# Retention attention with two MoE layers: two plain steps in layer 0, single-bank PSUM tiles, set differences in wide pieces, copies ahead of halves, later spills

## The chip, the core and the metric

The kernel runs on one core of one Trainium2 chip. The metric is the device time of one execution in microseconds (us); the median of three runs of the kernel before is 580.47 us (580.2 to 581.05).

## The reference, cut to what matters

```python
for t in range(S):                       # attention: B 2, H 8, S 768, D 64
    state = gamma * state + einsum('bhd,bhe->bhde', k[:, :, t], v[:, :, t])
    y[:, :, t] = scale * einsum('bhd,bhde->bhe', q[:, :, t], state)
x = y.transpose(0, 2, 1, 3).reshape(1536, 512)
h = x @ moe_w_in                          # 512 x 2048
x = (h * (1 / (1 + exp(-h)))) @ moe_w_out # layer 0, 2048 x 512
h = x @ moe2_w_in
out = maximum(0.01 * h, h) @ moe2_w_out   # layer 1
```

## The kernel before

Line numbers are those of the kernel before, whose code stands at the end of this section.

**Order.** The whole program is written by hand for one core (`manual_schedule`): each engine, and SyncE's DMA queue, takes its instructions in the order in which the code issues them. So an instruction that waits holds back everything behind it on its engine.

**Precision.** Each fp32 number is carried as two parts. `halves` (L177) makes them: ScalarE writes the high part h as a rounded copy (L178), then VectorE writes the low part l = s - h (L179). Each product takes three matmuls (`TERMS`: hh, hl, lh).

**Attention** (to about 58 us). Twelve chunks j of 128 positions. One turn of the loop (L537) gives TensorE `scores(j+1)` (L244), which needs queries that GpSimd has scaled (L222, for j of 5 and above), and `values(j)` (L264, L273, and L281 for the running state), which needs the scores that VectorE has masked (`masked`, L251). `store_x(j)` then splits the result y into halves for the up stage. Chunks 3 to 5 and 9 to 11 belong to the second half of a token group: `put_second` splits them in two pieces and forms on VectorE, chunk by chunk, the differences that Strassen's form needs (L318, L319, into `big`). `rest_t` (L324, L325) forms the other two on GpSimd. The table `behind` puts the preparation of the first weight blocks into the loop: `words` (ScalarE L131, L133), `clamp` (VectorE L137, L141), `sign` (L148), `low` (L155), then `split_a`.

**Layer, up stage.** Eight steps, one for each weight block. A step makes four output blocks g of two lanes (p0 and p1, 384 columns each). Step 0 is computed plainly by `begin` (96 matmuls, L648). Steps 1 to 7 take the Strassen-Winograd form (`rest`): 7 products of 12 matmuls (84, L376). They need sums of weight blocks (`sums`, GpSimd L175, then `split_s`) and of tokens (`split_t`, tiles tt0 and tt1). In a step several products accumulate into the same PSUM tile X, which ScalarE copies between them (`copy`, L405: tiles c0 to c2), and VectorE adds the copies to other tiles (`add`, L409). ScalarE applies the activation (`act`, L418 and L420). `keep` (L425) spills a step's g to DRAM.

**Layer, down stage.** Three sets of 512 tokens, each 8 times 24 matmuls of 512 columns (L453). A step's g is fetched back (`fetch_g`, L441) and split (`split_g`). Layer 0's result goes through `finish_x` (`put_first`, `put_second`) into the tiles that layer 1 reads.

**PSUM** is four pairs, p0 to p3, of two banks each. A pair is one tile: whoever waits for it waits for both banks.

## Time and profile before

| | |
|---|---|
| median of three runs | 580.47 us |
| the profiled execution | 580.35 us |
| its span | 578.6 us |
| TensorE (PE) busy | 555.2 us, 96% |
| VectorE (DVE) busy | 342.6 us, 59% |
| ScalarE (ACT) busy | 282.7 us, 49% |
| GpSimd (POOL) busy | 104.4 us, 18% |
| mean granted TensorE clock | 0.987 of full speed |

The profile lists the instructions of each engine with start and duration. The text in brackets at the end of a row says how long the engine had been idle before and who released it. PEclk is the granted clock of TensorE as a share of 2.4 GHz; 0.50 is 1.2 GHz.

### The profile page before, as it was taken

To read this page: it belongs to the slowest core of one execution; us is meant where nothing else is said; L and a number is where in the kernel's file an instruction comes from. 1 tells how busy PE (TensorE), PEld (TensorE's weight loads), DVE (VectorE), ACT (ScalarE), POOL (GpSimd) and SP (SyncE) were. 2 spreads that over 40 slices of the span, in tenths; PEclk is the share of its full clock that TensorE was granted. 3 is DMA by queue.
4 is the path that set the end of the run, shared out by engine and by line. 5 is a ranking of instruction groups with operands and counts; after the bars stand their busy time and mean duration, and the time that the engine had idled before them with its cause. 6 is when DMAs were issued, how large, how long until landed. Compare 5 with 4: busy or idle time off the path is not lost.

```text
span 578.6 us, 7971 instructions
## 1 busy us (share of the span) xinstructions
PE 555.2 (96%) x3246; PEld 498.1 (86%) x3246; DVE 342.6 (59%) x354; ACT 282.7 (49%) x330; POOL 104.4 (18%) x94
## 2 busy tenths in 40 slices
PE   8887979999998999999999899999999999999997
PEld 6776979999997888888888799999998888888885
DVE  4888866888865486676673756666655562212300
ACT  2223566777766565634622565566665453213201
POOL 2675433333300000000200532222200000000000
PEclk9988979999999999999999999999999999999999
DMA  8973216687876957878582075777627782532401
GB/s 323 392 269 116 73 36 219 228 290 283 289 257 237 374 188 215 292 228 311 189 260 105 0 261 175 249 258 252 223 110 290 283 293 94 167 109 84 137 0 73
DMA packets 35129, 119.09 MB, mean 206 GB/s; under 512 B 3218, under 2 KB 3346, under 8 KB 33044
## 3 DMA queue, kind: packets, MB, share of 16 engines
q1 hardware_dynamic: 34800, 118.24, 58.8%
q8 instruction: 25, 0.41, 0.3%
q10 hardware_dynamic: 292, 0.34, 0.2%
q14 instruction: 12, 0.10, 0.1%
HBM read 80.82 MB, written 37.75 MB: 205 GB/s over the span
## 4 chain that ended last, share of the span: by engine, by line
PE 83%; DVE 6%; DMA 5%; ACT 3%; POOL 1%; issue 1%; SPq 0%; DVEq 0%; ACTq 0%
PE p L453 44%; PE p L376 33%; DMA sf<-g 3%; DMA att_a<-att_dram 3%; PE p L648 2%; DVE w L179 2%; POOL sf L175 1%; PE p L273 1%; PE p L264 1%; ACT w L178 1%; PE p L244 1%; DVE c L251 1%; DVE r L155 1%; DVE big L318 1%; DVE big L319 1%
## 5 line engine op out<-in xcount | busy, mean ns | idle before, releaser
L376 PE MATMUL p<-tt,w 128*128 128x384 f32 x672 | 126.3, 340 | 3.7 <-ACT c L405 3.7
L376 PEld LDWEIGHTS p<-tt,w 128*128 128x128 f32 x672 | 119.4, 190 | 5.3 <-ACT c L405 5.2
L179 DVE TENSOR_TENSOR w<-c,w 128x1024 fp32r<-128x1024 f32 x46 | 56.2, 1224 | 90.2 <-ACT w L178 90.1
L453 PE MATMUL p<-w,wt 128*128 128x512 f32 x432 | 98.4, 389 | 0.0
L453 PE MATMUL p<-wt,w 128*128 128x512 f32 x432 | 98.4, 389 | 0.0
L453 PEld LDWEIGHTS p<-wt,w 128*128 128x128 f32 x432 | 81.1, 188 | 16.8
L453 PEld LDWEIGHTS p<-w,wt 128*128 128x128 f32 x432 | 81.1, 188 | 16.8
L178 ACT ACTIVATE w<-c 128x1024 fp32r<-128x1024 f32 x46 | 48.4, 1061 | 60.0 <-DMA c<-g 34.4
L453 PE MATMUL p<-w,w 128*128 128x512 f32 x288 | 67.3, 391 | 1.8 <-DVE w L179 1.0
L376 PE MATMUL p<-xa,w 128*128 128x384 f32 x336 | 64.3, 341 | 2.1 <-ACT big L418 2.1
L453 PEld LDWEIGHTS p<-w,w 128*128 128x128 f32 x288 | 53.8, 188 | 14.3 <-DVE w L179 2.2
L376 PEld LDWEIGHTS p<-xa,w 128*128 128x128 f32 x336 | 59.8, 190 | 2.5 <-ACT big L418 2.5
L409 DVE TENSOR_TENSOR big<-p,c 128x768 f32<-128x768 f32 x42 | 40.1, 954 | 32.3 <-PE p L376 19.8
L405 ACT ACTIVATE c<-p 128x768 f32<-128x768 f32 x42 | 34.1, 812 | 48.7 <-PE p L376 48.6
L175 POOL TENSOR_TENSOR sf<-r 128x256 f32<-128x256 f32 x28 | 33.9, 1232 | 115.6 <-DVE r L155 61.1
L133 ACT ACTIVATE u<-ws 128x1024 int32<-128x1024 uint32 x32 | 36.4, 1137 | 22.5 <-DVE r L155 22.5
L155 DVE CUSTOM_DVE_ANT_0 r<-r,u 128x2048 uint16<-128x2048 uint16 x32 | 41.2, 1289 | 0.9 <-ACT u L133 0.5
L131 ACT ACTIVATE r<-ws 128x1024 f32<-128x1024 f32 x32 | 36.6, 1143 | 9.7 <-DMA scr<-r 5.5
L179 DVE TENSOR_TENSOR w<-sf,w 128x1024 fp32r<-128x1024 f32 (+1 forms) x18 | 21.7, 1205 | 32.8 <-ACT w L178 32.8
L148 DVE SCALAR_TENSOR_TENSOR r<-ws,r 128x1024 int32<-128x1024 int32 x32 | 39.6, 1236 | 0.7
L324 POOL TENSOR_TENSOR big<-big 128x768 f32<-128x768 f32 x4 | 7.3, 1832 | 169.1 <-DVE big L319 169.1
L179 DVE TENSOR_TENSOR w<-r,w 128x768 fp32r<-128x768 f32 (+1 forms) x20 | 23.5, 1175 | 14.5 <-ACT w L178 14.5
(86 smaller groups left out, 566.0 us busy)
## 6 DMA issues: line engine op xcount, KB each, us to landing
ws<-w_dram SPq DMA_DIRECT2D x64, 512.0 KB, 5.7
g<-big SPq DMA_DIRECT2D x16, 1536.0 KB, 5.8
c<-g SPq DMA_DIRECT2D x46, 512.0 KB, 6.8
att_a<-att_dram SPq DMA_DIRECT2D x18, 512.0 KB, 6.4
scr<-r SPq DMA_DIRECT2D x18, 512.0 KB, 6.4
r<-scr SPq DMA_DIRECT2D x18, 512.0 KB, 7.4
att_b<-att_dram SPq DMA_DIRECT2D x6, 512.0 KB, 8.3
out_dram<-big SPq DMA_DIRECT2D x11, 256.0 KB, 2.1
```

Source lines behind the costliest of these rows:

```text
L131: nc.scalar.activation(out=r.bitcast(F32), in_=t[:, :, :, 1].bitcast(F32), func=AF.Abs)
L133: nc.scalar.activation(out=u, in_=t[:, :, :, 0].bitcast(U32), func=AF.Copy, scale=2.0 ** -29)
L148: nc.vector.scalar_tensor_tensor(out=r, in0=t[:, :, :, 1], scalar=-0x40000000, in1=r, op0=ALU.bitwise_and, op1=ALU.bitwise_or)
L155: nc.vector.tensor_tensor(out=r, in0=r, in1=u, op=ALU.add)
L175: nc.gpsimd.tensor_tensor(out=o, in0=a, in1=b, op=op)
L178: nc.scalar.activation(out=h, in_=s, func=AF.Copy)
L179: nc.vector.tensor_tensor(out=l, in0=s, in1=h.bitcast(F32), op=ALU.subtract)
L376: nc.tensor.matmul(out=o, lhsT=a[:, ta, k * 128:k * 128 + 128], rhs=rhs(p, tb, k), start=(begin and m == 0), stop=(end and m == 5), skip_g ...
L405: nc.scalar.activation(out=ct[n][:, c, 0:N], in_=self.X[:, c, 0:N], func=AF.Copy)
L409: nc.vector.tensor_tensor(out=self.block(f, half, lanes), in0=t[:, c, 0:N], in1=ct[n][:, c, 0:N], op=ALU.add)
L453: nc.tensor.matmul(out=y, lhsT=l, rhs=r, start=(i == 0 and f == 0 and n == 0), stop=(i == Q - 1 and f == 1 and n == 2),)
L648: nc.tensor.matmul(out=places[m][:, p, 0:N], lhsT=a[:, ta, r, k * 128:k * 128 + 128], rhs=x, start=(n_ == 0), stop=(n_ == 11), skip_group_ ...
```

## The change

**1. A second plain step.** Step 1 of layer 0 is plain as well (96 matmuls in place of 84). `plain` takes the place of `begin`. Its g goes into `big`, and step 0's g into the three c tiles, which the new `keep` spills in step 1. Product 1 of the next step and the copy of it come ahead of the last plain block.

**2. PSUM.** Pairs 2 and 3 become four single banks b0 to b3 (`bank`, `lanes_of`). In the attention y and the state's u lie in separate banks, and `state(j)` is issued between the halves. An `add` into the single banks is made of two instructions of 384 columns in place of one of 768, so each Strassen-Winograd step has six of them for three.

**3. Set differences.** The subtractions L318 and L319 go from `put_second`. `first_t` and `rest_t` make them for all three chunks at once (128x768). In layer 0 lane 0's four are on GpSimd, right behind the attention's last `queries`, and lane 1's on VectorE in steps 0 and 1. In layer 1 lane 0's are on GpSimd in the down stage before, and lane 1's in step 0, two on VectorE and two on GpSimd.

**4. Copies first.** `finish_x` has ScalarE copy the results out of PSUM whole, and the halves are made later from the copies in SBUF. In the attention ScalarE copies chunks 5 and above to `big` behind their halves (in the kernel before only those of the first half, L350).

**5. Last step of a layer.** Its products run in the order 6, 2, 7, 5, 4, 3 (before: 6, 2, 5, 7, 4, 3). The first g is fetched in step 6 and the second in the last step, step 6's spill comes behind the last step, and the first g is split early in the last step. One weight block's preparation goes from layer 1's step 0 to layer 0's down stage.

```diff
+    call = sb.tile([128, 3, 2, 512], F32, name="c")
+    ct = [call[:, i] for i in range(3)]
...
+    def bank(i):
+        return ps.tile([128, 512], F32, tag=f"b{i}", name=f"b{i}")
+
+
+    def lanes_of(i):
+        if i < 2:
+            t = pair(i)
+            return [t[:, 0], t[:, 1]], [(slice(0, 2), t)]
+        t = [bank(2 * i - 4), bank(2 * i - 3)]
+        return t, [(slice(n, n + 1), t[n].unsqueeze(1)) for n in range(2)]
...
+    PLAIN = ((0, 0, 0), (0, 0, 1), (1, 0, 0))
...
-        t = pair(2 + j % 2)
-        yu[j] = y, uu = t[:, 0], t[:, 1]
+        yu[j] = y, uu = bank(2 * (j % 2)), bank(2 * (j % 2) + 1)
...
-    def put_first(s, a, b, ys):
...
-        f, t = xf[p][:, :, :, a:b], tm[p][:, :, :, a:b]
-        h, l = (xb[p][:, n, :, a:b] for n in range(2))
-        halves(*(t[:, :, a:b] for t in b12[p]), ys[0])
...
-        nc.vector.tensor_tensor(out=t[:, 0], in0=ys[0], in1=f[:, 0], op=ALU.subtract)
-        nc.vector.tensor_tensor(out=t[:, 1], in0=ys[1], in1=t[:, 0], op=ALU.subtract)
-        halves(h, l, ys[1])
-
...
+
+
+    def first_t(p, e):
         f, t = xf[p], tm[p]
-        nc.gpsimd.tensor_tensor(out=f[:, 0], in0=t[:, 1], in1=f[:, 0], op=ALU.subtract)
-        nc.gpsimd.tensor_tensor(out=f[:, 1], in0=f[:, 1], in1=t[:, 1], op=ALU.subtract)
+        e.tensor_tensor(out=t[:, 0], in0=t[:, 0], in1=f[:, 0], op=ALU.subtract)
+        e.tensor_tensor(out=t[:, 1], in0=t[:, 1], in1=t[:, 0], op=ALU.subtract)
+
+    def rest_t(p, e):
+        f, t = xf[p], tm[p]
+        e.tensor_tensor(out=f[:, 0], in0=t[:, 1], in1=f[:, 0], op=ALU.subtract)
+        e.tensor_tensor(out=f[:, 1], in0=f[:, 1], in1=t[:, 1], op=ALU.subtract)
...
-        kept = False
+        y = g4(y)
+        f = (tm if s % 2 else xf)[s // 2][:, :, :, a:b]
...
+        if s % 2 == 0:
+            halves(*(xa[s // 2][:, n].rearrange("p (a k) n -> p a k n", a=2)[:, :, :, a:b] for n in range(2)), y)
+            state(j)
...
-            put_second(s, a, b, [y[:, 0], y[:, 1]])
+            halves(*put(s, a, b, 0)[0:2], y[:, 0])
+            state(j)
+            halves(*put(s, a, b, 1)[0:2], y[:, 1])
+        if j >= LATE:
+            nc.scalar.activation(out=f, in_=y, func=AF.Copy)
...
+        def go(self, n):
+            if n == 1:
+                self.X = lanes_of((self.i + self.layer) % 2)
+            if n == 2:
+                self.Z = lanes_of(2)
+            if n == 5:
+                self.V = lanes_of(3)
+            t = {2: "Z", 5: "V", 3: "V"}.get(n, "X")
+            for p, o in enumerate(getattr(self, t)[0]):
+                product(n, self.w, p, o[:, 0:N], n in (1, 2, 5), n in (2, 3, 4))
...
+        def add(self, f, half, n, t):
+            for c, t in t[1]:
+                nc.vector.tensor_tensor(
+                    out=self.block(f, half, c), in0=t[:, :, 0:N], in1=ct[n][:, c, 0:N], op=ALU.add
+                )
...
+            nc.sync.dma_start(out=t.rearrange("p f (s n) -> p f s n", s=4), in_=self.g)
...
+        for k, y in ((1, yb), (0, ya)):
+            for lo, hi, n, a in segments:
+                h, l, f = put(n, a, a + hi - lo, k)
+                for c, t in y[1]:
+                    nc.scalar.activation(out=f[:, c], in_=t[:, :, lo:hi], func=AF.Copy)
+                later.append((n, lambda h=h, l=l, f=f: halves(h, l, f)))
+        return [f for _, f in sorted(later, key=lambda t: t[0])]
...
         behind = {
-            2: lambda: load_next(), 5: lambda: load_next(),
+            2: load_next, 5: load_next,
             4: lambda: words(wa), 6: lambda: clamp(wa), 7: lambda: signed(wa),
-            8: lambda: low(wa), 9: lambda: split_a(wa),
-            10: lambda: (rest_t(0), words(wb)), 11: lambda: (rest_t(1), clamp(wb), signed(wb)),
+            8: lambda: low(wa), 9: lambda: split_a(wa), 10: lambda: words(wb), 11: lambda: clamp(wb),
...
             store_x(j)
-            state(j)
...
                 if k == 0:
-                    at(0, lambda: split_t(0, 0), lambda: low(wb))
-                    at(1, lambda: sums(wb), lambda: split_t(1, 0))
-                    at(2, lambda: split_a(wb))
-                    at(3, lambda: split_t(0, 1), lambda: words(wc))
-                    at(4, lambda: split_s(wb))
-                    at(5, lambda: split_t(1, 1))
+                    at(0, lambda: signed(wb), lambda: first_t(0, nc.gpsimd), lambda: rest_t(0, nc.gpsimd))
+                    at(1, lambda: low(wb))
+                    at(2, lambda: split_a(wb), lambda: words(wc))
+                    at(3, lambda: first_t(1, nc.vector))
+                    at(4, lambda: split_t(0, 0))
+                    at(5, lambda: split_t(1, 0))
                     at(6, lambda: clamp(wc), lambda: signed(wc))
                     at(7, lambda: low(wc), lambda: sums(wc))
                 else:
-                    at(0, lambda: split_a(wc))
-                    at(1, lambda: split_s(wc), lambda: words(wd))
-                    at(2, lambda: clamp(wd))
-                    at(3, lambda: signed(wd))
-                    at(4, lambda: low(wd), lambda: sums(wd))
+                    at(0, lambda: split_t(0, 1), lambda: rest_t(1, nc.vector))
+                    at(2, lambda: split_a(wc), lambda: words(wd))
+                    at(3, lambda: split_s(wc))
+                    at(4, lambda: split_t(1, 1), lambda: clamp(wd))
+                    at(5, lambda: signed(wd))
+                    at(6, lambda: low(wd), lambda: sums(wd))
...
             if k == 0:
-                at(0, lambda: split_t(1, 0), lambda: fetch_w(n))
-                at(2, lambda: split_a(n), lambda: words(w))
-                at(4, lambda: sums(n), lambda: clamp(w))
-                at(5, lambda: signed(w), lambda: fetch_w(m))
-                at(6, lambda: split_s(n), lambda: split_t(1, 1))
-                at(7, lambda: sums(m), lambda: (low(w), keep_w(w)))
+                at(0, lambda: fetch_w(n), lambda: first_t(1, nc.vector), lambda: rest_t(1, nc.gpsimd))
+                at(1, lambda: split_a(n))
+                at(2, lambda: split_t(1, 0))
+                at(4, lambda: sums(n), lambda: fetch_w(m))
+                at(6, lambda: split_s(n))
+                at(7, lambda: split_t(1, 1), lambda: sums(m))
...
-        def begin(s, n, tasks, tags, second_half, put_back):
+        def plain(s, n, before, tasks, tags, order, put_back):
...
+                    if before and p == 0 and at == 1:
+                        before.keep()
+                    f, half = ((0, 0), (1, 0), (0, 1), (1, 1))[m]
...
+                    for c, t in y[m][1]:
+                        if c.stop == p + 1:
+                            s.act(f, half, [(c, t)])
+                    if n and p == 1 and at == 2:
+                        n.go(1)
+                        n.copy(0)
                 put_back[p]()
-            n.go(1)
-            n.copy(0)
...
         def rest(s, n, before, tasks):
-            seq = (6, 2, 5, 7, 1, 4, 3) if n else (6, 2, 5, 7, 0, 4, 3)
+            seq = (6, 2, 5, 7, 1, 4, 3) if n else (6, 2, 7, 5, 4, 3)
             for m, p in enumerate(seq):
                 if m == 2:
-                    if before.i:
+                    if before.w not in PLAIN:
                         before.act(0, 1)
-                    before.keep()
-                if p == 7:
+                    if n:
+                        before.keep()
+                    else:
+                        fetch_g(s.layer, 0, 1)
+                if m == 3:
...
+                if m == 3:
                     s.add(1, 1, 2, s.V)
...
             for k in range(Q):
                 tasks = up_tasks(layer, k)
                 s, n = steps[k], steps[k + 1]
-                if k == 0:
-                    begin(s, n, tasks, ((0, 1, 2, 3), (1, 3, 0, 2))[layer],
-                          ((1, 0, 2, 3), (2, 0, 1, 3))[layer], put_back)
+                if s.w in PLAIN:
+                    more = n.w in PLAIN
+                    plain(s, None if more else n, steps[k - 1] if k else None, tasks,
+                          ((0, 1, 2, 3), (1, 3, 0, 2))[layer], ((0, 1, 2, 3), (0, 2, 1, 3))[layer],
+                          [lambda: None] * 2 if more else put_back)
                     s.done()
                     continue
                 if n is None:
                     ahead = second_w[layer][:2]
-                    tasks[2] += [lambda: fetch_g(layer, 0, 0), lambda: fetch_g(layer, 0, 1)]
-                    tasks[3] += [lambda: fetch_w(ahead[0])]
-                    tasks[4] += [lambda: split_g(layer, 0, 0), lambda: fetch_g(layer, 0, 2)]
-                    tasks[5] += [lambda: fetch_w(ahead[1])]
-                    tasks[6] += [lambda: split_g(layer, 0, 1)]
+                    tasks[1] += [lambda: split_g(layer, 0, 0)]
+                    tasks[2] += [lambda: fetch_w(ahead[0])]
+                    tasks[4] += [lambda: fetch_g(layer, 0, 2), lambda: fetch_w(ahead[1]), lambda: split_g(layer, 0, 1)]
+                elif k == Q - 2:
+                    tasks[4] += [lambda: fetch_g(layer, 0, 0)]
                 rest(s, n, steps[k - 1], tasks)
+            steps[Q - 2].keep()
             steps[Q - 1].act(0, 1)
             fetch_g(layer, 0, 3)
             steps[Q - 1].keep()
...
-                    finish_x(s, ya, yb)
-                    if s:
-                        rest_t(s - 1)
+                    later = finish_x(s, ya, yb)
+                    if s < 2:
+                        for m, f in enumerate(later):
+                            todo[n + 1 + m // 2].append(f)
+                    else:
+                        for f in later:
+                            f()
+                    if s == 1:
+                        todo[n + 3] += [lambda: first_t(0, nc.gpsimd), lambda: rest_t(0, nc.gpsimd)]
...
```

VectorE, attention, from the low words of the first weight block (L155 before, L167 now) to the masked scores of chunk 11 (the second L251 or L265); w1 and xb1 take chunk 9's halves, w2 the weight's. Before:

```order
L155 ISA r0_74<-r0_74,u_77 128x2048
L251 TENSOR_TENSOR c1_70<-p0_544,c0_69 128x1024
L179 TENSOR_TENSOR w1_87<-p3_555,w1_87 128x2x128
L318 TENSOR_TENSOR big_68<-p3_555,big_68 128x2x128
L319 TENSOR_TENSOR big_68<-p3_555,big_68 128x2x128
L179 TENSOR_TENSOR xb1_67<-p3_555,xb1_67 128x2x128
L294 TENSOR_TENSOR gst_84<-gst_84,p3_555 128x256
L179 TENSOR_TENSOR w2_88<-r0_74,w2_88 128x1024
L251 TENSOR_TENSOR c2_71<-p1_591,c0_69 128x1024
```

Now:

```order
L167 ISA r0_72<-r0_72,u_75 128x2048
L265 TENSOR_TENSOR c_69<-p0_546,c_69 128x1024
L191 TENSOR_TENSOR w1_85<-b2_557,w1_85 128x2x128
L307 TENSOR_TENSOR gst_82<-gst_82,b3_558 128x256
L191 TENSOR_TENSOR xb1_67<-b2_557,xb1_67 128x2x128
L191 TENSOR_TENSOR w2_86<-r0_72,w2_86 128x1024
L265 TENSOR_TENSOR c_69<-p1_593,c_69 128x1024
```

The two subtractions are gone and the state update (L294, now L307) stands ahead of the second half; the weight's low part still stands ahead of the masked scores.

TensorE at the change from plain blocks to the first Strassen-Winograd step of layer 0; its first product is p1_794 before and p0_911 now. Before:

```order
L648 MATMUL p3_664<-w1_87,w2_88 128x384 x6
L648 MATMUL p3_664<-xb1_67,w2_88 128x384 x6
L376 MATMUL p1_794<-xa0_64,w3_89 128x384 x6
L376 MATMUL p1_794<-xa1_65,w3_89 128x384 x6
L376 MATMUL p1_794<-tt0_85,w4_659 128x384 x6
L376 MATMUL p1_794<-tt1_658,w4_659 128x384 x6
```

Now:

```order
L654 MATMUL b1_795<-w1_85,w3_87 128x384 x6
L654 MATMUL b1_795<-xb1_67,w3_87 128x384 x6
L381 MATMUL p0_911<-xa0_64,w4_654 128x384 x6
L381 MATMUL p0_911<-xa1_65,w4_654 128x384 x6
L654 MATMUL b3_797<-w1_85,w3_87 128x384 x6
L654 MATMUL b3_797<-xb1_67,w3_87 128x384 x6
L381 MATMUL p0_911<-tt0_83,w5_655 128x384 x6
L381 MATMUL p0_911<-tt1_653,w5_655 128x384 x6
```

The first product's 12 matmuls moved ahead of the last plain block, which lies between them and the product with tt0.

ScalarE in the last up step of layer 0; sf holds the first g that is fetched back, r2 a weight block of the down stage. Before:

```order
L405 ACTIVATE c2_71<-p1_1492 128x2x384
L178 ACTIVATE w0_86<-r2_76 128x1024
L178 ACTIVATE w1_87<-sf_78 128x1024
L418 ACTIVATE big_68<-big_68 128x2x384
L418 ACTIVATE big_68<-p1_1492 128x2x384
L178 ACTIVATE w2_88<-c0_69 128x1024
```

Now:

```order
L413 ACTIVATE c_69<-p1_1532 128x2x384
L143 ACTIVATE r2_74<-ws1_71 128x1024
L145 ACTIVATE u_75<-ws1_71 128x1024
L190 ACTIVATE w5_655<-sf_76 128x1024
L426 ACTIVATE big_68<-big_68 128x2x384
L413 ACTIVATE c_69<-p1_1532 128x2x384
L426 ACTIVATE big_68<-big_68 128x2x384
L190 ACTIVATE w2_86<-r2_74 128x1024
L190 ACTIVATE w0_84<-c_69 128x1024
```

The split of the first g moved ahead of two activations, of the last copy and of the weight's split.

## Rows read from the trace of the kernel before

**Rows 1.** Waits of TensorE: who waited for whom, us, times, longest.

```profile
PE p L264 <- DVE c L251: 7.0, 4, 2.8
```

**Rows 2.** TensorE in time order, attention: start, us, line, tiles, [idle <-releaser].

```profile
26.97 1.09 PE L264 MATMUL p<-c,att_a 128*64 128x128 f32 x16 [1.33 <-DVE c L251]
...
33.02 1.09 PE L264 MATMUL p<-c,att_a 128*64 128x128 f32 x16 [2.24 <-DVE c L251]
...
46.84 1.09 PE L273 MATMUL p<-att_a,gst 64*64 64x128 f32 x16
...
55.16 1.98 PE L264 MATMUL p<-c,att_b 128*64 128x128 f32 x16 [2.76 <-DVE c L251]
57.06 1.68 PE L273 MATMUL p<-att_b,gst 64*64 64x128 f32 x16
```

**Rows 3.** TensorE in order of time, around the first Strassen-Winograd products of layer 0.

```profile
77.83 3.44 PE L376 MATMUL p<-xa,w 128*128 128x384 f32 x12 [2.14 <-ACT big L418]
82.18 3.91 PE L376 MATMUL p<-tt,w 128*128 128x384 f32 x12 [0.90 <-ACT c L405]
```

**Rows 4.** TensorE in order of time, ends of both up stages, layer 1.

```profile
181.44 2.35 PE L376 MATMUL p<-tt,w 128*128 128x384 f32 x12 [0.96 <-ACT c L405]
...
186.59 0.49 PE L453 MATMUL p<-w,w 128*128 128x512 f32 x1 [0.70 <-ACT w L178]
187.85 10.99 PE L453 MATMUL p<-w,w 128*128 128x512 f32 x47 [0.76 <-DVE w L179]
...
325.35 1.29 PE L648 MATMUL p<-b,w 128*128 128x384 f32 x6 [2.67 <-DVE xb L179]
...
338.01 2.25 PE L376 MATMUL p<-xa,w 128*128 128x384 f32 x12
341.15 2.38 PE L376 MATMUL p<-tt,w 128*128 128x384 f32 x12 [0.90 <-ACT c L405]
...
438.86 2.35 PE L376 MATMUL p<-tt,w 128*128 128x384 f32 x12 [0.96 <-ACT c L405]
```

**Rows 5.** Stretches: us; PE, PEld, DVE, ACT, POOL busy; PEclk; DMA share; GB/s.

```profile
34.40:37.80 3.40, 3.40 (x40) 2.95 (x38) 1.89 (x3) 1.10 (x3) 2.79 (x4) 0.50 0.89 334
54.90:58.30 3.40, 3.15 (x28) 2.81 (x30) 1.71 (x5) 2.04 (x3) 0.00 (x0) 0.50 0.02 5
78.70:85.60 6.90, 6.00 (x20) 5.49 (x19) 5.51 (x5) 4.14 (x6) 0.65 (x1) 0.51 0.12 36
90.00:170.00 80.00, 80.00 (x459) 79.90 (x458) 65.84 (x69) 60.34 (x70) 24.16 (x20) 1.00 0.74 260
```

**Rows 6.** VectorE in order of time, attention and layer 0's first step.

```profile
46.89 2.20 DVE L155 CUSTOM_DVE_ANT_0 r<-r,u 128x2048 uint16<-128x2048 uint16 x1
49.01 1.21 DVE L251 TENSOR_TENSOR c<-p,c 128x1024 f32<-128x1024 f32 x1
...
51.80 0.43 DVE L179 TENSOR_TENSOR xb<-p,xb 128x256 fp32r<-128x256 f32 x1 [0.45 <-ACT xb L178]
...
52.74 1.23 DVE L179 TENSOR_TENSOR w<-r,w 128x1024 fp32r<-128x1024 f32 x1 [0.20 <-ACT w L178]
...
68.07 1.22 DVE L155 CUSTOM_DVE_ANT_0 r<-r,u 128x2048 uint16<-128x2048 uint16 x1
```

**Rows 7.** GpSimd in order of time, attention.

```profile
27.96 1.28 POOL L222 TENSOR_TENSOR att_b<-att_b,gst 128x512 f32<-128x512 f32 x1 [1.49 <-DMA att_b<-att_dram]
...
46.20 1.81 POOL L324 TENSOR_TENSOR big<-big 128x768 f32<-128x768 f32 x1
47.97 2.80 POOL L325 TENSOR_TENSOR big<-big 128x768 f32<-128x768 f32 x1
```

**Rows 8.** ScalarE in order of time, attention.

```profile
51.38 0.38 ACT L178 ACTIVATE xb<-p 128x256 fp32r<-128x256 f32 x1 [2.41 <-DVE big L319]
51.66 1.05 ACT L178 ACTIVATE w<-r 128x1024 fp32r<-128x1024 f32 x1
```

**Rows 9.** Costliest groups: line, shapes, count, busy us, mean ns, idle before.

```profile
L409 DVE TENSOR_TENSOR big<-p,c 128x768 f32<-128x768 f32 x42 | 40.1, 954 | 32.3 <-PE p L376 19.8
```

More of the change, by code (lines that the diff above doesn't have):

```diff
@@ new lines, in copy, with act @@
+        def copy(self, n):
+            for c, t in self.X[1]:
+                nc.scalar.activation(out=ct[n][:, c, 0:N], in_=t[:, :, 0:N], func=AF.Copy)
+        def add(self, f, half, n, t):
[3 more added lines that the diff above has]
+                )
+        def act(self, f, half, t=None):
+            for c, i in [(slice(0, 2), None)] if t is None else t:
+                o = self.block(f, half, c)
+                i = o if i is None else i[:, :, 0:N]
+                if self.layer == 0:
+                    nc.scalar.activation(out=o, in_=i, func=AF.Silu)
+                else:
+                    nc.scalar.activation(out=o, in_=i, func=AF.Prelu, alpha=0.01)
@@ L541, in retention_moe_kernel @@
             if j == 0:
-                gb = pair(3)[:, 0]
+                gb = bank(2)
                 for r in range(2):
@@ L653, in begin @@
-                    if p == 1:
-                        s.act(f, half, places[m])
+                    todo = [(kk, ta, tb) for kk in range(4) for ta, tb in TERMS]
+                    for i, (kk, ta, tb) in enumerate(todo):
+                        x = xa[p][:, tb, kk] if half == 0 else b12[p][tb][:, kk] if kk < 2 else xb[p][:, tb, kk - 2]
+                        k = kk % 2
+                        nc.tensor.matmul(
+                            out=y[m][0][p][:, 0:N], lhsT=a[:, ta, (A11, A21)[f] + kk // 2, k * 128:k * 128 + 128],
+                            rhs=x, start=(i == 0), stop=(i == len(todo) - 1), skip_group_check=True,
+                        )
@@ L672, in rest @@
                     n.copy(0)
-                elif p:
+                else:
                     s.go(p)
```

128 lines of the change are left out of this document (34 added, 94 removed).

## The prediction

> **What bounds the kernel now.** Read the shares of the engines first: TensorE is busy for 96% of the 578.6 us span, so the end is set by how long TensorE works and by the few places where it waits. The waits of TensorE come next. The largest is the 7.0 us that the attention's value products wait for VectorE's masking, in four pieces [rows 1]. Then TensorE in order of time gives the place of each wait: 1.33, 2.24 and 2.76 us in the attention [rows 2], 2.14 and 0.90 at the first Strassen-Winograd step of layer 0 [rows 3], and in [rows 4] 0.96, 0.70 and 0.76 at the end of layer 0's up stage, 2.67 in layer 1's plain step, 0.90 behind it and 0.96 at the end of layer 1's up stage. Last, the stretches: from 90 to 170 us TensorE is busy for all 80.00 us, 459 matmuls of 0.174 each, with VectorE at 65.84, while in three short stretches the granted clock is at the lower level, 1.2 GHz [rows 5]. The first two of these come just after the waits that end at 33.02 and 55.16, the third during the two waits of [rows 3]. Twelve matmuls of a product take 2.25 us at full clock [rows 4] (at 338.01) and 3.44 and 3.91 in that third stretch [rows 3].
>
> The sum is made against the profiled execution, 580.35 us (span 578.6 and 1.75 around it), 0.12 below the median of the runs.
>
> **Attention.** Without the two subtractions, masked scores 5 and 6 leave VectorE earlier, and y's bank no longer waits for the state's matmuls. The waits of 1.33 and 2.24 go. In place of the second, GpSimd is late: its query product for chunk 7 waits for a transfer until 27.96 and takes 1.28 [rows 7], and TensorE, which would ask at about 28.3 (value products 5, now at 25.6, with the state's products behind them), waits some 0.97. So the chunks behind it come 1.33 + 2.24 - 0.97 = 2.6 us earlier. The lower clock from 34.40 to 37.80 cost half of 3.40 us [rows 5]; since a wait of 0.97 stays, I count half of that back, 0.85. Chunk 9's y, which ended at 46.84 + 1.09 = 47.93 [rows 2], then ends at 44.5.
>
> What is late next is chunk 11. Its masked scores still stand behind the split of the first weight block. From 44.5 the queue runs: ScalarE 0.38, VectorE 0.43, ScalarE 0.38, VectorE 0.43, ScalarE's whole copy (128x512: between 0.38 for 256 columns and 1.05 for 1024, I take 0.6), ScalarE's high part of the weight 1.05, VectorE's low part 1.23, masking 1.21 [rows 6, 8]. That is 5.7, and about 0.5 for hand-overs between the engines: 50.7. New beside it are GpSimd's four wide set differences, 1.81 each by [rows 7], right behind its last query product, so from about 43.5 to 51. Two VectorE operations of this queue read SBUF only: the low words and the weight's low part. Rows show what such a meeting does: the low words at 46.89 beside GpSimd's operation of 46.20 took 2.20, and 1.22 without one at 68.07; the masking at 49.01, whose input is in PSUM, took 1.21 although GpSimd's next operation ran [rows 6, 7]. So a meeting costs 0.98; at worst a whole GpSimd operation, 1.81, at best nothing. Two at 0.98 give 52.7 (bounds 50.7 and 54.3). Value products 11 start at 52.7 instead of 55.16: gain 2.46 (0.86 to 4.46). TensorE is idle longer ahead of them than before, so I leave the lower clock at the end of the attention as it was: 1.98 + 1.68 there [rows 2].
>
> The Trainium skill (SBUF — State Buffer, section "Who interferes with whom") speaks against this step: a VectorE instruction with two SBUF inputs and a GpSimd instruction that reads SBUF share a port pair that one holds for its whole instruction, and the later one is blocked fully. The trace agrees: 46.20 + 1.81 + 1.22 is 49.2, and the low words ended at 49.09; GpSimd's next operation took 2.80, having queued behind them. By this rule each meeting costs between 0 and 1.81, so the attention's gain would lie between the same bounds; without it, it would be 4.46.
>
> **Layer 0, up stage.** Twelve matmuls more: 84 become 96, 12 times 0.174 = +2.1 (2.25 with the fill, [rows 4]). The second plain step needs no sums of its weight block and no split tokens, so 16.7 us more of TensorE (96 times 0.174) go by before the first Strassen-Winograd step asks for any. Its first product waited 2.14 for the activation that frees its PSUM pair, queued on ScalarE behind a split that waited for GpSimd's sums. Now the sums are made well ahead. The pair's last block ends two blocks, 24 matmuls or 4.2 us, before product 1 asks; ScalarE has one activation to fit in, 0.8, at worst behind one token split of 1536 columns (about 1.5 on the line through 0.38 and 1.05 of [rows 8]) and one more activation. So the pair is free 1 to 3 us before TensorE asks. The 0.90 for the copy goes too: a plain block of 12 matmuls (2.1) now lies between product 1 and the next use of X, against a copy of 0.8 (768 columns on the same line). With both waits gone nothing precedes the third stretch of lower clock, so its 3.44 - 2.25 + 3.91 - 2.25 = 2.85 goes. Together 2.1 - 2.14 - 0.90 - 2.85 = -3.79. The bound on the bad side is that the pair comes late; that is a rival below.
>
> **The steady steps.** Six adds of 384 columns stand for three of 768, which took 0.954 each [rows 9]. No row shows 384 columns. Half of 0.954 and all of it are the ends, 0 to +2.9 a step on VectorE. Between 0.43 for 256 and 0.954 for 768 columns a line gives 0.55, which I take: +0.45 a step. A step is 84 times 0.174 = 14.6 us, and VectorE is busy for 65.84 of 80, so 12.0 of it [rows 5]: 2.6 of cover. Cost nothing.
>
> **Last step of layer 0.** With product 5 between 7 and 4 the copy after 7 has 2.1 us of cover: -0.96. The first g is fetched during step 6, so its split no longer waits for the transfer, and the down stage's first operand is ready: -0.70 - 0.76. SyncE's queue takes the first fetch ahead of the spill of step 6; behind it stand two weight fetches and the second fetch, which by the order are used two products or more later. Together -2.42 (bounds 0 and -2.42).
>
> **Layer 1.** Its third plain block waited 2.67 for PSUM that the subtractions and a split held. Six copies on ScalarE, 0.4 to 0.8 each by [rows 8], now free it within about 3.5 us, under two blocks of 4.2: -2.67. What they push back, the halves of the last set, is asked for by lane 1, four blocks or 8.4 us after the start. The 0.90 at 341.15 I leave: the copy now has a block's cover, but stands behind a weight split that waits for GpSimd's two differences and sums (bounds: it goes, -0.90, or grows by a GpSimd operation, +1.8). Its last step gains 0.96 as layer 0's does; I count the start of its down stage as unchanged. Moving the weight words to the down stage costs nothing, ScalarE being idle there.
>
> **Sum.** -2.46 - 3.79 - 2.42 - 2.67 - 0.96 = -12.3. 580.35 - 12.3 = 568.05, and 0.12 for the median: 568.2 us. Its own range is 565.5 to 571.
>
> **Rivals.**
> *Better attention.* No meeting and full clock: 2.0 less by the bound above, and 1.98 + 1.68 - 2 x 1.09 = 1.5 less [rows 2]: 564.7. For it: GpSimd may begin its differences late enough to miss the weight's low part. Against: the idle ahead of value products 11 grows.
> *The pair still late at step 2.* If ScalarE's activation of the second plain step waits for the token split, which itself waits for VectorE's differences beside GpSimd's sums, the wait returns at its old size with its lower clock: 2.14 + 2.85 = 5.0 more, 573.2. For it: that split stands directly ahead of the activation on ScalarE. Against: 1 to 3 us of slack.
> *Slower.* The single-bank adds cost what an operation costs that meets GpSimd, and VectorE sets the pace in layer 0's six Strassen-Winograd steps. At x us an add VectorE's work in a step is 12.0 - 2.86 + 6x; it exceeds 14.6 from x = 0.91, and the result is slower than before from 6 (9.14 + 6x - 14.6) = 12.3, so x = 1.25. At 0.55 + 0.98 = 1.53 it adds 22.3: 590.5. Against: their first input is in PSUM, as that of the masking which no meeting slowed.
> *The change does nothing.* The attention's transfers and the ports take back what the waits gave, and new waits stand at the layer ends: 580. The steps hold separately, so this needs all to fail.
>
> **Chances.** Forecast 0.58, better attention 0.17, pair late 0.17, slower 0.05, nothing 0.03. About 0.2% is what a measurement of this kernel tells from no change. So faster 0.92, same 0.03, slower 0.05. The range that holds the time 8 times in 10 reaches from the better attention to just above the late pair: 563.5 to 574.5.
>
> **What would show it.** Right: value products 11 start near 52.7; no idle before value products 5, 6 and 10, and about 1 us before score products 7; no wait and full clock at the first Strassen-Winograd step; no idle at the start of layer 0's down stage; layer 1's third plain block starts behind the second. Wrong: an idle of TensorE of more than 1 us anywhere between step 2 and the end of layer 0's up stage, adds above 0.9 us, or a stretch of lower clock in the two plain steps.

## The result and the profile after

The changed kernel takes 566.79 us (median of four runs, 566.38 to 569.15) against 580.41 for the kernel before: ratio 0.9772, 95% interval 0.9744 to 0.980. The forecast was 568.2 us, within 563.5 to 574.5. The profiled execution took 566.38, 13.97 less than that of before; the spans differ by 14.0 (578.6 and 564.6).

TensorE's share and instructions, from the page of the changed kernel:

```profile
PE 552.4 (98%) x3258; PEld 496.9 (88%) x3258; DVE 340.2 (60%) x377; ACT 285.9 (51%) x348; POOL 104.2 (18%) x92
```

TensorE in order of time, changed kernel. L258 is the attention's score products, L277 and L286 its value products, L654 the plain steps, L381 the Strassen-Winograd products, L458 the down stage:

```profile
29.08 1.16 PE L258 MATMUL p<-att_b 64*128 64x128 f32 x16 [0.79 <-POOL att_b L236]
...
41.82 1.16 PE L258 MATMUL p<-att_a 64*128 64x128 f32 x16 [0.96 <-POOL att_a L236]
...
51.53 1.09 PE L277 MATMUL b<-c,att_b 128*64 128x128 f32 x16 [2.72 <-issue]
...
54.19 5.42 PE L654 MATMUL p<-xa,w 128*128 128x384 f32 x24
59.45 1.23 PE L654 MATMUL b<-w,w 128*128 128x384 f32 x6
...
86.68 2.25 PE L381 MATMUL p<-xa,w 128*128 128x384 f32 x12
...
90.88 2.24 PE L381 MATMUL p<-tt,w 128*128 128x384 f32 x12
...
131.26 2.35 PE L381 MATMUL p<-tt,w 128*128 128x384 f32 x12 [0.40 <-ACT c L413]
...
176.35 2.35 PE L381 MATMUL b<-xb,w 128*128 128x384 f32 x12 [0.82 <-DVE big L417]
178.54 1.52 PE L458 MATMUL b<-w,w 128*128 128x512 f32 x6
...
195.67 1.20 PE L458 MATMUL b<-w,wt 128*128 128x512 f32 x4 [0.20 <-DVE wt L191]
...
207.70 1.20 PE L458 MATMUL b<-w,wt 128*128 128x512 f32 x4 [0.64 <-DVE wt L191]
...
310.74 2.25 PE L654 MATMUL p<-xa,w 128*128 128x384 f32 x12
...
314.90 1.20 PE L654 MATMUL p<-b,w 128*128 128x384 f32 x6
...
329.54 2.25 PE L381 MATMUL p<-tt,w 128*128 128x384 f32 x12
...
430.13 1.52 PE L458 MATMUL b<-w,w 128*128 128x512 f32 x6
...
559.33 1.52 PE L458 MATMUL b<-wt,w 128*128 128x512 f32 x6
```

The attention's waits of 1.33 and 2.24 [rows 2] are gone, and so are all of [rows 3] and the waits of 2.67, 0.90 and 0.96 in layer 1 [rows 4]. The wait of 2.76 ahead of value products 11 is left (2.72). Gone are also 0.70 and 0.76 at the start of layer 0's down stage; the 0.96 ahead of it gave way to 0.82. New in the attention are 0.79 and 0.96 for GpSimd's queries (and 0.38 at 38.12), new behind it 0.40, 0.82, 0.20 and 0.64, all in layer 0. Three rows of the kernel before complete the stage lengths:

```profile
62.95 1.23 PE L648 MATMUL p<-w,w 128*128 128x384 f32 x6
...
443.14 0.40 PE L453 MATMUL p<-w,w 128*128 128x512 f32 x1
...
559.72 15.12 PE L453 MATMUL p<-wt,w 128*128 128x512 f32 x66
```

| stretch, by starts on TensorE | before | after | change | forecast |
|---|---|---|---|---|
| up to the end of the first two plain blocks | 62.95 | 59.45 | -3.50 | -2.46 |
| from there to the first matmul of layer 0's down stage | 123.64 | 119.09 | -4.55 | -5.45 |
| layer 0's down stage | 131.77 | 132.20 | +0.43 | -0.76 |
| layer 1's up stage | 124.78 | 119.39 | -5.39 | -3.63 |
| layer 1's down stage to the last matmul's end | 131.70 | 130.72 | -0.98 | 0 |
| sum | | | -13.99 | -12.30 |

The sum was good to 1.7 us, but four of its rows missed by about 1 us each and one by 1.8, on both sides: the forecast gain was 3.8 us too small in three rows and 2.1 too large in two. That these partly cancel is luck.

Stretches of the changed kernel (us; busy time of the five engines; granted clock; DMA share; GB/s):

```profile
34.00:38.00 4.00, 3.74 (x64) 3.14 (x64) 3.97 (x4) 0.88 (x2) 3.36 (x3) 1.00 0.94 275
...
53.00:57.00 4.00, 4.00 (x22) 3.67 (x20) 0.94 (x3) 3.02 (x6) 0.74 (x1) 0.59 0.00 0
...
61.00:90.00 29.00, 29.00 (x168) 29.00 (x167) 23.39 (x19) 19.28 (x23) 7.40 (x7) 1.00 0.43 146
```

Of the three stretches of lower clock [rows 5] one is left, behind the 2.72 us idle. It now falls on the first plain blocks (5.42 us for 24 matmuls; the 24 at 63.66 took 4.33 at full clock).

### The profile page after: what moved, and what is told of

It reads as the page before. It is cut to its first block, busy times and chain, and to the rows that moved or that the text cites. A ratio compares the mean times of both kernels' runs of the same rounds, so it can differ in the third digit from the quotient of the medians.

```text
span 564.6 us, 8051 instructions
## 1 busy us (share of the span) xinstructions
PE 552.4 (98%) x3258; PEld 496.9 (88%) x3258; DVE 340.2 (60%) x377; ACT 285.9 (51%) x348; POOL 104.2 (18%) x92
## 2 busy tenths in 40 slices
DMA packets 35129, 119.09 MB, mean 211 GB/s; under 512 B 3218, under 2 KB 3346, under 8 KB 33044
## 4 chain that ended last, share of the span: by engine, by line
PE 81%; DMA 7%; DVE 5%; ACT 3%; issue 3%; POOL 1%; SPq 0%; ACTq 0%; POOLq 0%; DVEq 0%
PE b L458 23%; PE p L458 19%; PE p L381 15%; PE b L381 10%; PE p L654 5%; PE b L654 4%; DMA att_a<-att_dram 3%; DMA r<-scr 3%; PE p L258 1%; PE b L286 1%; PE b L277 1%; DVE big L417 1%; DMA scr<-r 1%; ACT w L190 1%; POOL sf L187 1%
## 5 line engine op out<-in xcount | busy, mean ns | idle before, releaser
L381 PE MATMUL p<-tt,w 128*128 128x384 f32 x468 | 88.1, 336 | 0.4 <-ACT c L413 0.4
L381 PEld LDWEIGHTS p<-tt,w 128*128 128x128 f32 x468 | 82.2, 188 | 0.7 <-ACT c L413 0.7
L458 PE MATMUL b<-wt,w 128*128 128x512 f32 x252 | 63.0, 389 | 0.0
L458 PE MATMUL b<-w,wt 128*128 128x512 f32 x216 | 55.6, 391 | 0.8 <-DVE wt L191 0.8
L458 PEld LDWEIGHTS b<-wt,w 128*128 128x128 f32 x252 | 47.3, 188 | 9.8
L458 PE MATMUL p<-w,wt 128*128 128x512 f32 x216 | 54.8, 389 | 0.0
L458 PEld LDWEIGHTS b<-w,wt 128*128 128x128 f32 x216 | 40.4, 188 | 10.2 <-DVE wt L191 1.6
L417 DVE TENSOR_TENSOR big<-b,c 128x384 f32<-128x384 f32 x78 | 40.3, 550 | 13.7 <-ACT c L413 7.2
L458 PEld LDWEIGHTS p<-w,wt 128*128 128x128 f32 x216 | 40.5, 188 | 8.5
L458 PE MATMUL p<-wt,w 128*128 128x512 f32 x180 | 46.5, 389 | 0.0
L167 DVE CUSTOM_DVE_ANT_0 r<-r,u 128x2048 uint16<-128x2048 uint16 x32 | 40.9, 1277 | 0.9 <-ACT u L145 0.2
L458 PEld LDWEIGHTS p<-wt,w 128*128 128x128 f32 x180 | 33.8, 188 | 7.0
L458 PE MATMUL b<-w,w 128*128 128x512 f32 x156 | 38.9, 389 | 0.0
L458 PEld LDWEIGHTS b<-w,w 128*128 128x128 f32 x156 | 29.3, 188 | 5.9
```

Of the source, the lines that this page charges most:

```text
L167: nc.vector.tensor_tensor(out=r, in0=r, in1=u, op=ALU.add)
L381: nc.tensor.matmul(out=o, lhsT=a[:, ta, k * 128:k * 128 + 128], rhs=rhs(p, tb, k), start=(begin and m == 0), stop=(end and m == 5), skip_g ...
L417: nc.vector.tensor_tensor(out=self.block(f, half, c), in0=t[:, :, 0:N], in1=ct[n][:, c, 0:N], op=ALU.add)
L458: nc.tensor.matmul(out=y, lhsT=l, rhs=r, start=(i == 0 and f == 0 and n == 0), stop=(i == Q - 1 and f == 1 and n == 2),)
```

## The experiments

Each is the changed kernel with the edit shown. Medians of the same kernel differ by chance by about 1 us (the kernel before: 579.93 to 580.93 beside these runs), so the stage lengths of the traces carry the verdicts (us, by starts on TensorE). "Start" is the start of step 0, and "blocks" the time from there to the end of the first two plain blocks, where the lower clock behind the attention can still fall; "L0 up" begins behind them. The start itself moves by chance: the changed kernel, e1_keep6, e2_seq and e3_late have the same code up to there and differ by 0.9, as TensorE waits 0.48 to 1.25 for chunk 10's queries, which wait for a transfer.

| run | median, ratio to before (95%) | start | blocks | L0 up | L0 down | L1 up | L1 down |
|---|---|---|---|---|---|---|---|
| before | 580.41 | 58.67 | 4.28 | 123.64 | 131.77 | 124.78 | 131.70 |
| changed | 566.79, 0.9772 (0.9744-0.980) | 54.19 | 5.26 | 119.09 | 132.20 | 119.39 | 130.72 |
| e1_keep6 | 564.71, 0.9747 (0.9727-0.9767) | 54.30 | 5.39 | 119.13 | 130.56 | 119.42 | 130.72 |
| e2_seq | 567.37, 0.9791 (0.9769-0.9813) | 55.09 | 4.68 | 120.43 | 131.31 | 120.66 | 130.72 |
| e3_late | 569.76, 0.9831 (0.9812-0.985) | 55.08 | 5.39 | 120.50 | 131.73 | 121.10 | 130.72 |
| e4_subs | 567.78, 0.9784 (0.9758-0.9809) | 56.40 | 4.27 | 119.73 | 132.05 | 119.42 | 130.72 |
| e5_wa | 564.25, 0.9739 (0.972-0.9758) | 50.43 | 4.27 | 121.28 | 131.81 | 119.42 | 130.73 |
| e6_port | 568.40, 0.9795 (0.9765-0.9825) | 52.54 | 4.29 | 124.02 | 132.12 | 119.41 | 130.73 |
| e7_one | 570.71, 0.9832 (0.9806-0.9858) | 55.90 | 4.29 | 123.74 | 131.45 | 119.69 | 130.73 |
| e9_best | 562.57, 0.9706 (0.9671-0.9742) | 50.85 | 4.27 | 120.19 | 131.79 | 119.40 | 130.77 |
| e10_best | 560.26, 0.9657 (0.9634-0.968) | 50.37 | 4.29 | 118.35 | 132.40 | 119.40 | 130.72 |

**e1_keep6: the late spill.**

```diff
-                    if n:
-                        before.keep()
-                    else:
+                    before.keep()
+                    if not n:
                         fetch_g(s.layer, 0, 1)
...
-            steps[Q - 2].keep()
```

> The changed kernel with one edit: step 6's spill goes back to its old place, ahead of the last step's third product, in both layers. Theory A: the two new waits in layer 0's down stage (TensorE's starts show 0.36 and 1.01 us lost there, 1.37 together) come from the 1.5 MB spill, now issued at 178 us just as the down stage begins, which takes transfer time from the fetches of g and of the weight blocks. Then they go, and the time is about 1.4 lower, 565.4 (down to 565.0 if layer 1 gains too). Rival B: they come from the place of the splits on ScalarE and VectorE, whatever the transfers do; then the time stays within 0.3 of 566.8. Rival C: the spill ahead of the second fetch makes the first splits of the down stage wait again, 0.70 and 0.76 as before the change; then 568.0 or more.

SyncE and ScalarE of the changed kernel: the spill goes out at 178.05 with the down stage, and ScalarE waits 3.16 for a g, with the weight's split (wt) behind it in its queue:

```profile
178.05 1.18 SPq L432 DMA_DIRECT2D g<-big  x1
```

```profile
197.34 1.06 ACT L190 ACTIVATE w<-c 128x1024 fp32r<-128x1024 f32 x1 [3.16 <-DMA c<-g]
198.55 1.07 ACT L190 ACTIVATE wt<-r 128x1024 fp32r<-128x1024 f32 x1
```

The same two in e1_keep6:

```profile
193.62 1.07 ACT L190 ACTIVATE w<-c 128x1024 fp32r<-128x1024 f32 x1 [0.61 <-DMA c<-g]
195.28 1.06 ACT L190 ACTIVATE wt<-r 128x1024 fp32r<-128x1024 f32 x1 [0.59 <-DMA r<-scr]
```

The down stage is 1.64 shorter and both of TensorE's waits are gone, with the splits in the same order: theory A. From 163 us to the down stage the DMA share is 0.55 in the changed kernel and 0.68 in e1_keep6, in its first 16.5 us 1.01: the spill had room ahead of the stage and none in it. This part of the change cost time.

**e2_seq: the last step's order.**

```diff
-            seq = (6, 2, 5, 7, 1, 4, 3) if n else (6, 2, 7, 5, 4, 3)
+            seq = (6, 2, 5, 7, 1, 4, 3) if n else (6, 2, 5, 7, 4, 3)
```

> The changed kernel with one edit: the last step's products in the old order 6, 2, 5, 7, 4, 3, all else as changed. Theory A: in layer 0 the new order exchanged the copy's wait (0.96) for a wait of product 3 for the VectorE add (0.82 at 176.35), so undoing it costs nothing there, and about 1.1 in layer 1, where the new order has no wait: 567.9. Rival B: the 0.82 has another origin and stays; then the old order costs 1.1 in each layer: 569.0.

In layer 0 product 4 waits for the copy again, now 1.68, and product 3 no longer for the add (TensorE, then ScalarE, e2_seq):

```profile
175.90 2.37 PE L381 MATMUL p<-tt,w 128*128 128x384 f32 x12 [1.68 <-ACT c L413]
```

```profile
174.30 0.84 ACT L426 ACTIVATE big<-big 128x768 f32<-128x768 f32 x1 [1.49 <-DVE big L417]
175.05 0.79 ACT L413 ACTIVATE c<-p 128x768 f32<-128x768 f32 x1
```

Layer 0's up stage is 1.34 longer: 0.43 of it is a longer wait at 132.01 (as 131.26 above; 0.82 for 0.40), which lies ahead of the edit and differs as much between runs with equal code there (0.27 in e1_keep6), and about 0.9 the last step. Layer 1's is 1.27 longer. So the order was worth 0.9 in layer 0, near the price of rival B, but not in B's way, as the 0.82 did not stay; theory A had the exchange of the two waits right and their sizes wrong. The wait is longer than the 0.96 of the kernel before because the copy (175.05) now stands behind an activation that waits for an add on VectorE.

Why product 3 waits in the new order, VectorE of the changed kernel shows: the add that it waits for (175.75; its input was ready when product 5 ended near 173.4) stands behind a clamp and a sign:

```profile
172.22 1.01 DVE L417 TENSOR_TENSOR big<-b,c 128x384 f32<-128x384 f32 x2
173.16 0.68 DVE L149 TENSOR_SCALAR r<-r 128x1024 f32<-128x1024 f32 x1
173.88 0.69 DVE L153 TENSOR_SCALAR r<-r 128x1024 int32<-128x1024 int32 x1
174.60 1.23 DVE L160 SCALAR_TENSOR_TENSOR r<-ws,r 128x1024 int32<-128x1024 int32 x1
175.75 1.01 DVE L417 TENSOR_TENSOR big<-b,c 128x384 f32<-128x384 f32 x2
```

**e3_late: the first product behind the last plain block.**

```diff
-                    if n and p == 1 and at == 2:
-                        n.go(1)
-                        n.copy(0)
                 put_back[p]()
+            if n:
+                n.go(1)
+                n.copy(0)
```

> The changed kernel with one edit: the first product of the next step and its copy go back behind the last plain block, in both layers. Theory A: the copy (0.81) is uncovered again, 0.9 to 1.05 in each layer, 2.0 together, and the wait of 2.14 for the PSUM pair does not return since the pair is free long before: 568.8, with full clock in the first Strassen-Winograd step. Rival B: the early product is what removed the long wait; then 2.14 and the lower clock (2.85) come back too: 573 or more. Rival C: in layer 1 the copy stands behind a weight split that waits for GpSimd, so that only layer 0's 0.9 shows: 567.7.

TensorE in e3_late, in order of time and its waits for the copies:

```profile
92.94 2.38 PE L381 MATMUL p<-tt,w 128*128 128x384 f32 x12 [0.90 <-ACT c L413]
```

```profile
PE p L381 <- ACT c L413: 2.9, 3, 1.4
```

Layer 0's up stage is 1.41 longer and layer 1's 1.71. The 2.14 did not come back: theory A, with layer 1 dearer (1.4) than thought. So the early first product is also what removed layer 1's 0.90.

**e4_subs: differences chunk by chunk.**

```diff
...
             halves(*put(s, a, b, 0)[0:2], y[:, 0])
+            x = xf[s // 2][:, :, :, a:b]
+            t = tm[s // 2][:, :, :, a:b]
+            nc.vector.tensor_tensor(out=t[:, 0], in0=y[:, 0], in1=x[:, 0], op=ALU.subtract)
+            nc.vector.tensor_tensor(out=t[:, 1], in0=y[:, 1], in1=t[:, 0], op=ALU.subtract)
             state(j)
...
-        if j >= LATE:
+        if j >= LATE and s % 2 == 0:
             nc.scalar.activation(out=f, in_=y, func=AF.Copy)
...
```

(`first_t` is no longer called in layer 0; the second half's copies on ScalarE go too, and its chunks below `LATE` pass through `sf`)

> The changed kernel with the set differences of the attention made chunk by chunk on VectorE between the halves again, as before the change (and no wide first pair on GpSimd or VectorE); banks, copies and the rest stay as changed. Theory A: the wide pieces carry the attention's gain. Masked scores 5 and 6 leave late again, so waits of about 1.3 and 2 return, and chunk 11's queue is two subtractions (0.9) longer: value products 11 start near 54.5 in place of 51.53, and the time is about 569.5. Rival B: the separate banks carry it, because y no longer waits for the state's matmuls; then only the 0.9 shows: 567.7.

TensorE, e4_subs:

```profile
26.84 1.09 PE L277 MATMUL b<-c,att_a 128*64 128x128 f32 x16 [1.33 <-DVE c L265]
...
32.40 1.09 PE L277 MATMUL b<-c,att_a 128*64 128x128 f32 x16 [1.74 <-DVE c L265]
...
36.15 1.09 PE L277 MATMUL b<-c,att_b 128*64 128x128 f32 x16
...
52.74 1.95 PE L277 MATMUL b<-c,att_b 128*64 128x128 f32 x16 [2.56 <-DVE c L265]
```

The waits are back, 1.33 unchanged and 1.74 for 2.24, and value products 7 start at 36.15 for 33.92 in the changed kernel: 2.2 later, where all the other runs of the changed attention lie within 33.31 to 34.23. So the wide pieces, with the copies that went along, take these two waits away. What that is worth at the attention's end is not shown: value products 11 start only 1.2 later, not 3, as TensorE then waits less for chunk 10's queries (0.55 for 0.96), and their start alone differs from 50.49 to 51.89 between the changed kernel, e1_keep6, e2_seq and e3_late. The time lies near B, but B has the wrong waits. Value products 7 start at 38.31 in the kernel before; the rest of that gain is with the clock, which stayed at its full level behind the 1.74 (before, it was at 0.50 from 34.40 to 37.80), the separate banks and the place of `state`, which no run took apart.

**e5_wa: the weight split behind chunk 11's masking.**

```diff
-            8: lambda: low(wa), 9: lambda: split_a(wa), 10: lambda: words(wb), 11: lambda: clamp(wb),
+            8: lambda: low(wa), 10: lambda: words(wb), 11: lambda: clamp(wb),
...
                 masked(j + 1)
+            if j == 10:
+                split_a(wa)
             store_x(j)
```

> The changed kernel with one edit: the split of the first weight block comes behind the masked scores of chunk 11 instead of ahead of them, on ScalarE and VectorE. Theory A: the idle of 2.72 ahead of value products 11 goes since masking ends at about 48.0, before TensorE asks at 48.75; the weight's low part ends at about 50.3, before step 0 asks at 50.9; so step 0 starts 3.3 us earlier, and with no idle ahead the lower clock around 53 to 57 (about 1.7 us of cost) goes too: 562.0 (563.5 if the clock falls all the same). Rival B: step 0 now waits for the weight split beside GpSimd's differences, and only 1 us or less is left: 566.

No idle before value products 11; step 0 starts at 50.43, 3.76 earlier, and the granted clock is 1.00 throughout. The blocks are 1.0 shorter for it. But layer 0's up stage is 2.2 longer, through waits that stood there small or not at all (TensorE, e5_wa):

```profile
82.44 2.36 PE L381 MATMUL p<-xa,w 128*128 128x384 f32 x12 [0.35 <-ACT big L426]
112.70 2.37 PE L381 MATMUL p<-tt,w 128*128 128x384 f32 x12 [0.55 <-ACT c L413]
128.69 2.35 PE L381 MATMUL p<-tt,w 128*128 128x384 f32 x12 [1.04 <-ACT c L413]
```

Theory A's place, not its size: 2.5 of 4.8 us stayed.

**e6_port: no GpSimd beside the weight's low part.**

```diff
-                    at(0, lambda: signed(wb), lambda: first_t(0, nc.gpsimd), lambda: rest_t(0, nc.gpsimd))
+                    at(0, lambda: signed(wb))
...
-                    at(3, lambda: first_t(1, nc.vector))
+                    at(3, lambda: first_t(0, nc.vector), lambda: rest_t(0, nc.gpsimd), lambda: first_t(1, nc.vector))
```

> The changed kernel with lane 0's set differences taken away from the attention's end: the first two go to VectorE in step 0 of layer 0, the other two stay on GpSimd behind them, so GpSimd is idle while VectorE makes the weight's low part. Theory A: that low part took 1.90 instead of 1.23 because it met a GpSimd operation; then it takes 1.23, value products 11 start 0.67 earlier after chunk 9's end (6.50 between chunk 9's last L286 row's end and their start becomes 5.8), and the time is 566.1; the lower clock around 53 to 57 stays, since the idle ahead of it stays above 2 us. Rival B: the low part is slow for another reason (ScalarE writing the same tile) and stays at 1.9: 566.8.

The low part on VectorE and GpSimd's operation beside it in the changed kernel, then the low part in e6_port, and TensorE and ScalarE in e6_port:

```profile
48.40 1.90 DVE L191 TENSOR_TENSOR w<-r,w 128x1024 fp32r<-128x1024 f32 x1 [1.61 <-ACT w L190]
```

```profile
47.41 1.81 POOL L329 TENSOR_TENSOR big<-big 128x768 f32<-128x768 f32 x1
```

```profile
48.03 1.23 DVE L191 TENSOR_TENSOR w<-r,w 128x1024 fp32r<-128x1024 f32 x1 [1.61 <-ACT w L190]
```

```profile
50.49 1.09 PE L277 MATMUL b<-c,att_b 128*64 128x128 f32 x16 [2.05 <-issue]
...
86.30 3.69 PE L381 MATMUL p<-xa,w 128*128 128x384 f32 x12 [2.07 <-ACT big L426]
```

```profile
82.73 1.06 ACT L190 ACTIVATE w<-sf 128x1024 fp32r<-128x1024 f32 x1 [3.22 <-POOL sf L187]
```

From the end of chunk 9's y (43.57 + 1.09) to 50.49 are 5.83, where the changed kernel took 6.50: the meeting cost 0.67, theory A. The Trainium skill (SBUF — State Buffer, "Who interferes with whom") says that a VectorE instruction with two SBUF inputs contends with a GpSimd instruction that reads SBUF. The trace agrees: 47.41 + 1.81 + 1.23 is 50.45, and the low part ended at 50.30. The clock did not fall behind the 2.05 idle, against the expectation. And the run shows a rival of the prediction at work: with the differences moved into the plain steps, the activation that frees the PSUM pair stands on ScalarE behind a weight split that waits 3.22 for GpSimd's sums. TensorE's wait is 2.07 (2.14 before), and the product behind it runs at the lower clock, 3.69 (3.44 before). Layer 0's up stage is 4.9 longer (a wait at 133.53 grew to 1.36 too) and the kernel is slower than the changed one.

**e7_one: one plain step.**

```diff
-    PLAIN = ((0, 0, 0), (0, 0, 1), (1, 0, 0))
+    PLAIN = ((0, 0, 0), (1, 0, 0))
```

(step 0's and 1's side work comes in an order that suits it, step 0's activations all come in the second lane, and its g goes into `big`)

> The changed kernel with only step 0 of layer 0 plain, as before the change (12 matmuls fewer, step 1 in Strassen-Winograd form, step 0's activations all in the second lane); the early first product, the wide differences and the rest stay. Theory A: the first Strassen-Winograd step waits again for sums and splits, about as long as before (2.14 or more) and with the lower clock behind it (2.85), less 2.1 for the matmuls: about +2.9, 569.7. Rival B: GpSimd's sums now stand behind its four wide differences, so that the wait is longer: 572 or more. Rival C: the early first product alone covers the wait, and the second plain step only adds its 12 matmuls: 564.7.

TensorE and ScalarE, e7_one:

```profile
43.24 2.08 PE L258 MATMUL p<-att_a 64*128 64x128 f32 x16 [3.42 <-POOL att_a L236]
...
73.94 3.77 PE L381 MATMUL p<-xa,w 128*128 128x384 f32 x12 [3.10 <-ACT big L423]
...
91.77 2.35 PE L381 MATMUL p<-tt,w 128*128 128x384 f32 x12 [1.50 <-ACT c L410]
```

```profile
73.08 0.81 ACT L423 ACTIVATE big<-p 128x768 f32<-128x768 f32 x1 [2.37 <-DVE big L334]
```

The wait for the pair is back, 3.10, and the lower clock with it, but by another way than theory A has it: the activation that frees the pair waits for a set difference on VectorE (L334), while the weight split behind the sums had started at 69.64. Layer 0's up stage takes 4.65 more with 12 matmuls (2.1) fewer, so the new waits and the clock cost 6.7, the 1.50 at 91.77 among them; A had 5.0. The wait is longer, as B has it, but not for B's reason. What the second plain step gives is the time in which this preparation is done. The order of the side work is mine, so the size holds for this order only. The late start (55.90) comes with the 3.42 at 43.24, a wait for chunk 10's queries in the attention, whose code is unchanged.

**e9_best and e10_best: together.** e9_best joins the edits of e1_keep6 and e5_wa with this one:

```diff
-                    at(2, lambda: clamp(w))
-                    at(3, lambda: signed(w))
+                    if k + 1 < Q:
+                        at(2, lambda: clamp(w))
+                        at(3, lambda: signed(w))
+                    else:
+                        at(4, lambda: clamp(w), lambda: signed(w))
```

> Three edits together on the changed kernel: step 6's spill back at its old place (its run took 1.6 us off layer 0's down stage), the first weight block's split behind the masked scores of chunk 11 (its run took 2.5), and in layer 0's last step the clamp and sign of a weight block on VectorE behind the add that product 3 waits for (0.82 and the restart, about 1). Theory A: they stand in different stages and add up: 566.8 - 1.6 - 2.5 - 1.0 = 561.7. Rival B: what comes earlier runs into the transfers, and a third or more is lost in new waits: 563.5 or more.

562.57 lies between the two expectations. The 0.82 is gone; the down stage's gain is mostly not: it takes 131.79 (130.56 in e1_keep6), and TensorE arrives there 3.5 us earlier. e10_best adds these:

```diff
-                    at(3, lambda: split_s(wc))
-                    at(4, lambda: split_t(1, 1), lambda: clamp(wd))
+                    at(3, lambda: split_t(1, 1))
+                    at(4, lambda: split_s(wc), lambda: clamp(wd))
...
-                    at(2, lambda: words(w, (0,)), lambda: clamp(b))
-                    at(3, lambda: words(b, (1,)), lambda: signed(b), lambda: clamp(w))
-                    at(4, lambda: (low(b), sums(b)))
-                    at(5, lambda: words(w, (1,)), lambda: signed(w))
+                    at(2, lambda: clamp(b))
+                    at(3, lambda: words(b, (1,)), lambda: signed(b))
+                    at(4, lambda: words(w, (0,)), lambda: (low(b), sums(b)))
+                    at(5, lambda: clamp(w), lambda: words(w, (1,)), lambda: signed(w))
```

> The three edits of the run before and two more against the waits that the second of them brought into layer 0's up stage (0.35, 0.55 and 1.04): the token split of lane 1 comes ahead of the weight split that waits for GpSimd's sums, and ScalarE takes the high words of the second weight block, which wait for a spill, behind the copy that TensorE needs. Theory A: those waits are queueing on ScalarE and go, about 2 us with their restarts: 559.7. Rival B: the waits are set by the transfers, and move to another instruction: within 0.5 of the run with three edits.

The three waits that e5_wa brought are gone and layer 0's up stage is 1.84 shorter than in e9_best: theory A, for the two edits together. The median is 560.26, faster than both kernels of the case. What is left on TensorE behind the attention (e10_best):

```profile
168.70 2.37 PE L381 MATMUL p<-tt,w 128*128 128x384 f32 x12 [0.56 <-ACT c L413]
185.19 1.20 PE L458 MATMUL b<-w,wt 128*128 128x512 f32 x4 [0.64 <-DVE wt L191]
202.33 1.21 PE L458 MATMUL b<-w,wt 128*128 128x512 f32 x4 [0.44 <-DVE wt L191]
```

The down stage's waits are back although the spill is early. In its first 17 us the DMA share is 0.96, so an earlier TensorE may meet the transfers there; but it is 0.99 in e1_keep6, which has no wait. e9_best's own edit is a rival: as VectorE's clamp and sign come later, ScalarE's split of the second weight block starts 1.2 us behind the down stage's start (174.22), in e1_keep6 0.6 ahead of it (178.21). The two were not tried apart.

## Why the prediction was right, point by point

- *Attention, -2.46 forecast, -3.50 measured.* The chain was right: chunk 11's masking behind the weight's split, at 51.53 for 52.7. Mis-sized was the term of two meetings at 0.98. Only one counted, at 0.67 (e6_port); the delay of the low words ended before y was there. Against that, y of chunk 9 ended at 45.03 for 44.5. The wait for the query product of chunk 7 came as said (0.79 for 0.97), others for later chunks stood beside it. One of the prediction's signs of being wrong did show, a stretch of lower clock in the plain steps: it is the one behind value products 11, whose cost was left in the sum and fell in part into step 0 (about 1.6 us with the value products, 1.5 before).
- *Layer 0's up stage.* The pair's wait, the copy's wait and the lower clock went. e3_late brings the copy's wait back, e6_port the pair's with the lower clock, by the sums as the prediction had it, and e7_one both of these by the set differences. The steady steps did not change: the 384-column add took 0.550, as worked out (0.55), which ends the slower rival.
- *End of layer 0's up stage, -0.96: wrong.* The step "the copy after 7 has 2.1 us of cover" held, but product 3 then waited for the add behind VectorE's weight work. I looked at the queue of ScalarE only. With the old order the stage would have been 0.9 longer still (e2_seq).
- *Layer 0's down stage, -0.76 at its start and else unchanged: wrong in the second half.* The 0.76 went as said. The step that placed the late spill "behind" the first fetches counted the queue and not what the 1.5 MB takes from transfers still needed (e1_keep6).
- *Layer 1, -3.63 forecast, -5.39 measured.* The 0.90 went too, by the early first product. And a wait costs more than its idle: 24 matmuls from 318.36 at 0.174 end at 322.54, the next started at 325.35 [rows 4], 2.81 for an idle of 2.67. By the starts of single matmuls, with the slower one that follows each wait, the waits of 2.67, 0.90 and 0.96 cost 2.91, 1.17 and 1.23, together 5.3 of this row, and nearly all of the 0.98 in the down stage is two waits of the kernel before that are gone, at 443.14 (0.53) and 449.17 (0.37).
- *Rivals.* "Pair late" did not come in the changed kernel, but moving four operations brings it (e6_port), through GpSimd's sums and not through the token split. "Better attention" came in part: one meeting fewer, clock still low at the end.
